# Set-up of a clustered-attention kernel: the first head pair's mask rows written by engines in place of transfers

## The chip, the cores and the metric

The kernel runs on one core of one Trainium2 chip. The metric is device time in microseconds (us) of one execution, the median of several runs; lower is better. The profile is of one execution of its own.

## What is computed

Clustered attention over 2 batches of 8 heads (768 positions, 64 wide), then two mixer blocks. Queries and keys are assigned to the nearest of 16 centroids, and a query sees only keys of its own cluster:

```
q_assign = np.argmax(np.einsum('bhsd,hcd->bhsc', q_n, c_n), axis=-1)
k_assign = np.argmax(np.einsum('bhsd,hcd->bhsc', k_n, c_n), axis=-1)
mask = q_assign[:, :, :, None] == k_assign[:, :, None, :]
scores = np.where(mask, scale * np.matmul(q, k.transpose(0, 1, 3, 2)), -1000000000.0)
attn = softmax(scores)
x = attn @ v                                  # then, with x as [batch, seq, 512]:
u = x + (x.T @ U @ V).T;  x = u + relu(u @ w_ch1) @ w_ch2
u = x + (relu(x.T @ w_tok1) @ w_tok2).T;  out = u + relu(u @ w_ch1') @ w_ch2'
```

## The kernel before

Heads are taken in pairs: 2 batches of 4 pairs, 8 pairs in all, and the head dimension of a pair lies on 128 partitions (head 0 on 0 to 63, head 1 on 64 to 127). float32 products are made of rounded high and low parts (`rnd`, line 75, writes the high part; `sub`, line 84, the low), and high and low rows are stacked into one contraction, so that a score tile takes two matmuls per half of the keys. For this each head of a pair has two operand tiles, `qS[g % 2][a]` and `kS[g % 2][a]` (a = head; the tiles lie in `qk0` and `qk1`, which the profile shows as qk). Rows 0 to 63 of a tile (for head 1, 64 to 127) hold the head itself; the other half holds 32 crossed rows at a time, copied there from other partitions by DMA (`cross`, line 253). Sixteen rows more carry the mask (`stack(..., "mask", ...)`, lines 270 to 273): a one-hot of the query's cluster on the query side, and 0 or -2^100 on the key side, so that a score of another cluster is pushed below every other.

The one-hots come from `scores` (line 193: centroids against q and k, four matmuls into one bank), `scores_out` (DVE transposes, tile am), `arg0` to `arg4` (lines 208 to 232: largest score, weights that settle a tie, compare, transpose into ohT) and `mask_rows` (line 234, into om), from which eight small DMAs per pair write the mask rows.

After `setup()` (line 390) the attention runs as 96 steps (`step`, line 659), 12 per pair, one score tile of 128 queries each. Step n issues the score matmuls of tile n+2 (`s_mm`), their maximum on DVE (`s_max`, line 294), the exponential of tile n+1 on ACT (`s_exp`, line 298), six transposes of tile n on PE (`t_mm`, line 313), their copies to pt (`t_out`, every third on DVE), and, from step 6 on, in odd steps the products with v (`pv`). A score bank is used again two tiles later, so the matmuls of tile n+2 wait for the exponential of tile n. Work for later pairs hangs on the steps by tables: `late[n]`, `acts[n]`, `low[n]`, `mid[n]` (line 588 on) are run at fixed places of step n. Every engine and every queue runs its instructions in the order in which they are written.

The second pair's raw q and k lie in pt (`raw1`, line 180, four blocks of 768 columns: raw q, high q, raw k, high k), which the softmax copies overwrite from step 6 on. SP's queue carries nearly all transfers, in program order: the first pair's crossed rows, the second pair's stack ("hi", "lo", "mask"), the third pair's load, v, then V and U (`load_uv`, line 497) and the weights. U is turned from 64-bit to float32 by ACT and DVE in place of the host (`uv`, line 502; on ACT at `acts[11]`, on DVE in `late[12]`).

`busy(n)` (line 447) issues n transposes of the identity into an unused bank.

## Time and profile before

| | |
|---|---|
| median of 3 runs | 754.79 us (754.76 to 754.88) |
| profiled execution | 754.72 us |
| its span in the profile | 752.9 us |
| PE busy | 739.8 us (98%) |
| DVE, ACT, POOL busy | 466.9, 311.6, 164.9 us |
| chain that ended last | PE 94%; DVE 2%; DMA, ACT, SP's queue 1% each |

The span is what the profile covers; the execution's own time is 1.8 us longer. Engines: PE makes matmuls and transposes, DVE, ACT and POOL work on elements, SP only issues transfers. Times within the execution count from the span's start. A line number in a row (L73) is that of the kernel before, often of a helper.

### The profile page before, as it was taken

What the parts mean: (1) busy time and instruction counts of PE and PEld (TensorE: products, weight loads), DVE (VectorE), ACT (ScalarE), POOL (GpSimd) and SP (SyncE); (2) the same over time, 40 slices, a digit from 0 to 9 for tenths busy, and PEclk for the clock granted to TensorE, in tenths of its full rate; (3) what the DMA queues carried; (4) which work ended last, traced back from release to release, by engine and by line L of the source; (5) the groups of instructions that cost most, each with busy time, mean ns of one, the idle gap of its engine ahead of it and who ended that gap; (6) DMA issues with size and microseconds to landing.
All of it is one profiled execution on the core that took longest, in us unless ns stands there. A gap on an engine that the chain in (4) does not pass through costs nothing.

```text
span 752.9 us, 10578 instructions
## 1 busy us (share of the span) xinstructions
PE 739.8 (98%) x3901; PEld 586.3 (78%) x3901; DVE 466.9 (62%) x690; ACT 311.6 (41%) x565; POOL 164.9 (22%) x145
## 2 busy tenths in 40 slices
PE   6999999999999999999999999999999999999998
PEld 4766766777776788888888888888888888888886
DVE  7788988878875567956667777567675331122113
ACT  5868778767776333322332334233232310101010
POOL 5132153232111122412212222136021410000000
PEclk9999999999999999999999999999999999999999
DMA  5797588785312354554433799878796538556652
GB/s 167 197 220 194 143 214 214 207 207 116 73 53 117 112 207 186 218 201 193 172 108 115 261 365 364 306 236 284 253 321 206 196 113 299 195 185 214 229 191 84
DMA packets 51715, 149.40 MB, mean 198 GB/s; under 512 B 7792, under 2 KB 15984, under 8 KB 49616
## 3 DMA queue, kind: packets, MB, share of 16 engines
q1 hardware_dynamic: 51104, 147.81, 61.4%
q10 hardware_dynamic: 560, 0.92, 0.4%
q8 instruction: 31, 0.51, 0.3%
q14 instruction: 20, 0.16, 0.1%
HBM read 97.32 MB, written 32.51 MB: 172 GB/s over the span
## 4 chain that ended last, share of the span: by engine, by line
PE 94%; DVE 2%; DMA 1%; ACT 1%; SPq 1%; issue 1%; DVEq 0%
PE ps L73 84%; PE ps L318 8%; PE ps L381 1%; PE ps L850 1%; PE ps L338 1%; DVE nm L296 1%; DMA sq__81<-in_qT_dram 1%; DMA qk<-pt 1%; ACT p L301 0%; SPq L256 0%; ACT pt L325 0%; DVE p L440 0%; ACT qk L78 0%; DVE u_sb L100 0%; SPq L263 0%
## 5 line engine op out<-in xcount | busy, mean ns | idle before, releaser
L754 DVE SCALAR_TENSOR_TENSOR gl<-ps,gh 128x512 fp32r<-128x512 f32 x84 | 58.0, 691 | 209.6 <-ACT gh L753 209.6
L753 ACT ACTIVATE gh<-ps 128x512 fp32r<-128x512 f32 x84 | 50.3, 598 | 312.8 <-PE ps L73 312.8
L73 PE MATMUL ps<-gh,qk 128*128 128x512 f32 x544 | 179.5, 391 | 0.1
L73 PEld LDWEIGHTS ps<-gh,qk 128*128 128x128 f32 x544 | 102.1, 188 | 21.6 <-issue 0.5
L73 PE MATMUL ps<-qk 112*128 112x384 f32 (+2 forms) x456 | 108.9, 365 | 1.4 <-DMA qk<-om 0.7
L296 DVE TENSOR_REDUCE nm<-ps 128x1 f32<-128x768 f32 x96 | 91.5, 955 | 28.2 <-PE ps L73 25.4
L73 PE MATMUL ps<-gl,qk 128*128 128x512 f32 x272 | 106.0, 390 | 0.0
L301 ACT ACTIVATE p<-ps,nm 128x768 f32<-128x768 f32 x96 | 86.1, 899 | 27.0 <-DVE nm L296 26.2
L85 POOL TENSOR_TENSOR qk<-c__77,qk 128x512 fp32r<-128x512 f32 x40 | 54.9, 1381 | 191.2 <-ACT qk L78 163.4
L318 PEld LDWEIGHTS ps<-ident,p 128*128 128x128 f32 x576 | 68.2, 140 | 34.0 <-issue 26.9
L318 PE MATMUL ps<-ident,p 128*128 128x128 f32 x576 | 91.2, 277 | 1.3 <-DVE pt L323 0.8
L73 PEld LDWEIGHTS ps<-qk 112*128 112x128 f32 (+1 forms) x456 | 76.2, 190 | 9.4 <-ACT p L301 3.6
L73 PE MATMUL ps<-u2h,qk 128*128 128x512 f32 x224 | 73.9, 391 | 0.0
L73 PE MATMUL ps<-pt,vr 128*64 128x384 f32 x384 | 72.1, 498 | 0.0
L325 ACT COPY pt<-ps 128x512 f32<-128x512 f32 x96 | 55.7, 587 | 26.9 <-PE ps L318 26.4
L73 PEld LDWEIGHTS ps<-gl,qk 128*128 128x128 f32 x272 | 51.1, 188 | 10.3
L73 PE MATMUL ps<-u1h,qk 128*128 128x512 f32 x160 | 52.6, 390 | 0.0
L100 DVE TENSOR_SCALAR c__77<-c__77 128x512 f32<-128x512 f32 (+2 forms) x47 | 48.9, 1041 | 0.8 <-ACT c__77 L96 0.7
L73 PEld LDWEIGHTS ps<-u2h,qk 128*128 128x128 f32 x224 | 42.1, 188 | 8.6
L109 DVE SCALAR_TENSOR_TENSOR c__77<-c__76,c__77 128x512 int32<-128x512 int32 (+2 forms) x47 | 43.4, 924 | 1.5
L106 DVE SCALAR_TENSOR_TENSOR c__77<-c__76,c__77 128x512 int32<-128x512 int32 (+2 forms) x47 | 43.5, 925 | 1.1
L73 PE MATMUL ps<-u2l,qk 128*128 128x512 f32 x112 | 43.6, 390 | 0.0
(153 smaller groups left out, 1027.1 us busy)
## 6 DMA issues: line engine op xcount, KB each, us to landing
qk<-scr_b SPq DMA_DIRECT2D x72, 512.0 KB, 3.5
c__76<-in_wa_dram SPq DMA_DIRECT2D x16, 1024.0 KB, 4.9
qk<-scr_a SPq DMA_DIRECT2D x32, 512.0 KB, 7.5
c__76<-in_wb_dram SPq DMA_DIRECT2D x24, 512.0 KB, 5.6
scr_b<-qk SPq DMA_DIRECT2D x24, 512.0 KB, 4.8
scr_a<-wx SPq DMA_DIRECT2D x16, 512.0 KB, 3.0
scr_a<-qk SPq DMA_DIRECT2D x16, 512.0 KB, 3.2
qk<-sq__81 SPq DMA_DIRECT2D x12, 384.0 KB, 4.1
```

Of the source, the lines that this page charges most:

```text
L73: pe.matmul(o, lhsT=l, rhs=r, start=start, stop=stop, **kw)
L85: eng.tensor_tensor(out=o, in0=a, in1=b, op=ALU.subtract)
L100: dve.tensor_scalar(out=dst, in0=dst, scalar1=2.0 ** -15, scalar2=122879.9921875, op0=ALU.max, op1=ALU.min)
L106: dve.scalar_tensor_tensor(out=d, in0=lo, scalar=29, in1=d, op0=ALU.logical_shift_right, op1=ALU.bitwise_or)
L109: dve.scalar_tensor_tensor(out=d, in0=hi, scalar=-0x40000000, in1=d, op0=ALU.bitwise_and, op1=ALU.bitwise_or)
L296: dve.tensor_reduce(out=nm[:, n % 4 : n % 4 + 1], in_=ps[:, b0 : b0 + 2, 0:HS], axis=AX.XY, op=ALU.max, negate=True)
L301: act.activation(p32[n % NP32].rearrange("p (j k) -> p j k", j=2), ps[:, b0 : b0 + 2, 0:HS], AF.Exp, bias=nm[:, n % 4 : n % 4 + 1], accum_ ...
L318: pe.transpose(ps[:, tb[j], ts(i, P)], p32[n % NP32][:, ts(c, P)], ident)
L325: act.copy(o, ps[:, tb[j], :])
L338: pe.transpose(ps[:, bk, ts(t, P)], osb[q % 2][:, ts(t, P)], ident)
L753: act.activation(gh, o, AF.Relu)
L754: dve.scalar_tensor_tensor(out=gl, in0=o, scalar=0.0, in1=f32(gh), op0=ALU.max, op1=ALU.subtract)
```

## The change

In `setup()`:

- The first pair's mask rows are no longer written to om and moved by eight DMAs. DVE (`k_row`) and ACT or POOL (`q_row`) write them straight from the transposed one-hots into the operand tiles, 16 partitions at a time.
- The end of the argmax is made for each head by itself: `eq` compares half the elements (one head's columns) into am3 or a new tile amb, of which the other half stays zero, and a transpose follows for each (ohT for head 0, ohb for head 1). Head 0's rows come first.
- Head 1's low parts of q and k go from DVE to POOL, behind a copy of one element (`turn`) that waits for head 0's last key row; POOL also scales raw q for it ahead.
- ACT rounds head 0's q in two pieces, with k between; the exponential's table is loaded ahead of the second pair's rounding, not behind it.
- Two of POOL's four fills go behind this work, the iota ahead of all of them.
- `busy` is issued in three places: 22 transposes as soon as the identity is there (before: none), 32 behind the cluster scores (44), 9 behind the first score matmuls (12).

In the tables of the steps: the second pair's `scores_out` and `arg0` move from the set-up to steps 0 and 1, head 1's second key row to step 0, the second pair's low parts, `arg2` to `mask_rows` and their DMAs from steps 0 to 3 to steps 4 to 6, and U and V from step 6 to 8. `raw1` takes its blocks in another order, so that the high parts are overwritten first.

```diff
-    raw1 = tuple(pt[:, 2 * NBL * P + i * S : 2 * NBL * P + (i + 1) * S] for i in range(4))
+    raw1 = tuple(pt[:, 2 * NBL * P + i * S : 2 * NBL * P + (i + 1) * S] for i in (2, 0, 3, 1))
...
+            busy(22)
             dve.memset(zc, 0.0)
-            for i in range(NST):
-                for t in (qS, kS):
-                    pool.memset(f32(t[i][1])[32:64], 0.0)
             wi = tmp.tile([P, 16], F32, name="wi")
             pool.iota(wi, pattern=[[-1, 16]], base=16, channel_multiplier=0, allow_small_or_imprecise_dtypes=True)
+            for t in (qS, kS):
+                pool.memset(f32(t[0][1])[32:64], 0.0)
+            amb = tmp.tile([P, HS], BF16, name="amb")
+            for x in (am3, amb):
+                dve.memset(x, 0.0)
...
-            for a in range(2):
-                m, _, _ = rows(a)
-                q, k = qS[0][a], kS[0][a]
-                rnd(act, q[m], Rq[m].unsqueeze(1).to_broadcast([64, 2, S]), 0.125)
-                rnd(act, k[m, 1, :], Rk[m])
-                if a == 0:
-                    cross(f32(k), f32(k[:, 1, :]), a, sp)
-                    low_q(0)
-                    low_k(0, pool)
-                else:
-                    cross(f32(k), f32(k[:, 1, :]), a, sp)
+            q, k = qS[0], kS[0]
+            pool.tensor_scalar(out=l[64:128], in0=Rq[64:128], scalar1=0.125, scalar2=None, op0=ALU.mult)
+            rnd(act, q[0][0:64, 0, :], Rq[0:64], 0.125)
+            rnd(act, k[0][0:64, 1, :], Rk[0:64])
+            rnd(act, q[0][0:64, 1, :], Rq[0:64], 0.125)
+            cross(f32(k[0]), f32(k[0][:, 1, :]), 0, sp)
+            dve.scalar_tensor_tensor(out=l[0:64].bitcast(F32R), in0=Rq[0:64], scalar=0.125, in1=f32(q[0][0:64, 0, :]),
+                                     op0=ALU.mult, op1=ALU.subtract)
+            cross(f32(q[0]), l, 0, sp)
+            sub(pool, k[0][0:64, 0, :], Rk[0:64], f32(k[0][0:64, 1, :]))
+            rnd(act, q[1][64:128], Rq[64:128].unsqueeze(1).to_broadcast([64, 2, S]), 0.125)
+            rnd(act, k[1][64:128, 1, :], Rk[64:128])
+            cross(f32(k[1]), f32(k[1][:, 1, :]), 1, sp)
+            act.activation(tiny, n1, AF.Exp, scale=0.0)
             scores(0)
             scores(1, raw1)
-            busy(44)
-            q_hi(raw1)
-            k_hi(raw1)
-            act.activation(tiny, n1, AF.Exp, scale=0.0)
+            busy(32)
             scores_out(0)
             arg0()
             arg1(dve)
             arg2()
-            arg3(dve)
-            arg4()
-            mask_rows(dve)
-            for a in range(2):
-                stack(0, a, "mask", (act, sp))
-            low_q(1)
-            low_k(1, dve)
-            for a in range(2):
-                stack(1, a, "hi", sp, raw1)
-            scores_out(1)
-            arg0()
-            arg1(pool)
-            k_lo(pool, raw1)
-            s_mm(0)
-            s_mm(1)
-            busy(12)
-            s_max(0)
-            s_max(1)
+            w3, wb_, v24 = (x.rearrange("p (g a c) -> p g a c", a=2, c=16) for x in (am3, amb, am2))
+            b24 = amx.rearrange("p (g a) -> p g a", a=2).unsqueeze(3).to_broadcast([P, 12, 2, 16])
+
+            def eq(o, a):
+                dve.tensor_tensor(out=o[:, :, 0, :], in0=v24[:, :, a, :], in1=b24[:, :, a, :], op=ALU.is_equal)
+
+            def k_row(a, oh, h):
+                y = rows(a)[2]
+                dve.tensor_scalar(out=k[a][y, 0, ts(h, HS)], in0=oh[64 + 32 * h : 80 + 32 * h], scalar1=-1.0, scalar2=BIG,
+                                  op0=ALU.add, op1=ALU.mult)
+
+            def q_row(eng, a, oh, h):
+                y = rows(a)[2]
+                o, i = q[a][y, 0, ts(h, HS)], oh[32 * h : 32 * h + 16]
+                if eng is act:
+                    act.activation(o, i, AF.Copy)
+                else:
+                    eng.tensor_copy(o, i)
+
+            eq(w3, 0)
+            dve.transpose(out=ohT, in_=am3)
+            for h in range(2):
+                k_row(0, ohT, h)
+                q_row(act, 0, ohT, h)
+            q_hi(raw1)
+            k_hi(raw1)
+            eq(wb_, 1)
+            dve.transpose(out=ohb, in_=amb)
+            pool.tensor_copy(tmp.tile([16, 1], F32, name="turn"), f32(k[0][96:112, 0, S - 1 : S]))
+            sub(pool, l[64:128].bitcast(F32R), l[64:128], f32(q[1][64:128, 0, :]))
+            cross(f32(q[1]), l, 1, sp)
+            q_row(pool, 1, ohb, 0)
+            sub(pool, k[1][64:128, 0, :], Rk[64:128], f32(k[1][64:128, 1, :]))
+            q_row(pool, 1, ohb, 1)
+            s_mm(0)
+            s_mm(1)
+            busy(9)
+            s_max(0)
+            s_max(1)
+            k_row(1, ohb, 0)
+            for a in range(2):
+                stack(1, a, "hi", sp, raw1)
+            late[0].insert(0, lambda: k_row(1, ohb, 1))
+            for t in (qS, kS):
+                pool.memset(f32(t[1][1])[32:64], 0.0)
+            k_lo(pool, raw1)
...
-    for s, f in ((0, lambda: q_lo(dve, raw1)), (1, arg2), (2, lambda: arg3(dve)), (2, arg4), (3, lambda: mask_rows(dve))):
+    for s, f in ((0, lambda: scores_out(1)), (1, arg0), (1, lambda: arg1(pool)), (4, lambda: q_lo(dve, raw1)), (5, arg2),
+                 (5, lambda: arg3(dve)), (6, arg4), (6, lambda: mask_rows(dve))):
```

On DVE, from the weights of the argmax to the second pair's first piece (am_83 is am, am_84 and am_85 are am2 and am3, qk_72 the first pair's operand tiles, nm the maxima), before:

```order
L222 TENSOR_REDUCE amx<-am_84 128x24
L229 TENSOR_TENSOR am_85<-am_84,amx 128x384
L232 STREAM_TRANSPOSE ohT<-am_85 128x384
L235 TENSOR_SCALAR om<-ohT,msk 128x384
L440 SCALAR_TENSOR_TENSOR p_3_94<-sq__81,qk_72 64x768
L85 TENSOR_TENSOR qk_72<-sk__82,qk_72 64x768
L201 STREAM_TRANSPOSE am_83<-ps 128x384
L209 TENSOR_REDUCE amx<-am_83 128x24
L296 TENSOR_REDUCE nm<-ps 128x1 x3
```

and with the change:

```order
L223 TENSOR_REDUCE amx<-am_84 128x24
L471 TENSOR_TENSOR am_85<-am_84,amx 128x12x16
L487 STREAM_TRANSPOSE ohT<-am_85 128x384
L475 TENSOR_SCALAR qk_72<-ohT 16x384 x2
L471 TENSOR_TENSOR amb<-am_84,amx 128x12x16
L494 STREAM_TRANSPOSE ohb<-amb 128x384
L297 TENSOR_REDUCE nm<-ps 128x1 x2
L475 TENSOR_SCALAR qk_72<-ohb 16x384
L297 TENSOR_REDUCE nm<-ps 128x1
```

Two low parts and the second pair's transpose and reduction have left the stretch ahead of the first maxima; head 1's key rows stand between maxima.

On POOL, from head 0's low k part to the second pair's argmax, before:

```order
L404 MEMSET qk_73 32x1536 x2
L406 IOTA wi 128x16
L85 TENSOR_TENSOR qk_72<-sk__82,qk_72 64x768
L85 TENSOR_TENSOR am_83<-am_83,amx 128x384
L215 TENSOR_SCALAR am_84<-am_83 128x384
L216 TENSOR_TENSOR am_84<-am_84,wcl 128x384
L85 TENSOR_TENSOR pt<-pt 128x768
```

and with the change:

```order
L447 TENSOR_SCALAR p_3_95<-sq__81 64x768
L85 TENSOR_TENSOR qk_72<-sk__82,qk_72 64x768
L495 COPY turn<-qk_72 16x1
L85 TENSOR_TENSOR p_3_95<-p_3_95,qk_72 64x768
L484 CAST qk_72<-ohb 16x384
L85 TENSOR_TENSOR qk_72<-sk__82,qk_72 64x768
L484 CAST qk_72<-ohb 16x384
L511 MEMSET qk_73 32x1536 x2
L85 TENSOR_TENSOR pt<-pt 128x768
L85 TENSOR_TENSOR am_83<-am_83,amx 128x384
```

POOL has a full row of work between the first pair's low k part and the second pair's argmax, where there was none.

On SP's queue, behind the second pair's high parts (qk_73 are that pair's tiles), before:

```order
L267 DMA qk_73<-pt 64x768
L256 DMA qk_73<-pt 32x768 x2
L267 DMA qk_73<-pt 64x768
L256 DMA qk_73<-pt 32x768 x2
L184 DMA sq__81<-in_qT_dram 128x768
L185 DMA sk__82<-in_kT_dram 128x768
L272 DMA qk_73<-om 16x384
```

and with the change:

```order
L185 DMA sq__81<-in_qT_dram 128x768
L186 DMA sk__82<-in_kT_dram 128x768
L190 DMA vr_91<-in_v_dram 128x6x128
L268 DMA qk_73<-pt 64x768
L257 DMA qk_73<-pt 32x768 x2
L268 DMA qk_73<-pt 64x768
L257 DMA qk_73<-pt 32x768 x2
L273 DMA qk_73<-om 16x384
```

The third pair's load and the second v, which stood before and behind the mask rows, now go ahead of the low parts; eight mask rows, V and U follow in both.

## Rows read from the trace of the kernel before

**Rows 1.** The page's busy time and share of each engine.

```profile
PE 739.8 (98%) x3901; PEld 586.3 (78%) x3901; DVE 466.9 (62%) x690; ACT 311.6 (41%) x565; POOL 164.9 (22%) x145
```

**Rows 2.** Chain of waits, 0 to 52 us: start, length, what it went through.

```profile
29.52 0.97 PE ps L73 x4
```

**Rows 3.** Timeline, DVE, set-up: start, length, line, operation, out<-in, count [idle before].

```profile
9.46 0.86 DVE L218 TENSOR_TENSOR am<-am,amx 128x384 bf16<-128x384 f32 x1
...
11.34 0.56 DVE L229 TENSOR_TENSOR am<-am,amx 128x384 bf16<-128x384 bf16 x1
11.93 0.58 DVE L232 STREAM_TRANSPOSE ohT<-am 128x384 bf16<-128x384 bf16 x1
12.54 0.48 DVE L235 TENSOR_SCALAR om<-ohT,msk 128x384 f32<-128x384 bf16 x1
13.05 0.95 DVE L440 SCALAR_TENSOR_TENSOR p<-sq__81,qk 64x768 fp32r<-64x768 f32 x1
...
16.50 1.82 DVE L296 TENSOR_REDUCE nm<-ps 128x1 f32<-128x768 f32 x2 [0.42 <-PE ps L73]
```

**Rows 4.** Timeline, POOL, set-up.

```profile
8.06 1.85 POOL L85 TENSOR_TENSOR qk<-sk__82,qk 64x768 fp32r<-64x768 f32 x1 [1.08 <-ACT qk L78]
...
17.09 1.18 POOL L215 TENSOR_SCALAR am<-am 128x384 bf16<-128x384 f32 x1
```

**Rows 5.** Timeline, PE, set-up.

```profile
9.43 5.28 PE L449 MATMUL ps<-ident 128*128 128x128 f32 x44
15.39 1.78 PE L73 MATMUL ps<-qk 112*128 112x384 f32 x8 [0.68 <-DMA qk<-om]
```

**Rows 6.** Timeline, ACT, set-up.

```profile
5.76 1.49 ACT L78 ACTIVATE qk<-sq__81 64x1536 fp32r<-64x1536 f32 x1 [2.02 <-DMA sq__81<-in_qT_dram]
...
11.83 1.28 ACT L467 ACT_TABLE_LOAD   x1
...
13.12 0.20 ACT L467 ACTIVATE tiny<-n 128x1 f32<-128x1 f32 x1
```

**Rows 7.** Busy time by stretch: length, then PE, PEld, DVE, ACT, POOL, PEclk, DMA.

```profile
16.50:31.00 14.50, 13.33 (x87) 11.12 (x85) 12.14 (x16) 10.30 (x22) 4.39 (x4) 1.00 0.88 202
```

**Rows 8.** Timeline, DVE, steps 0 and 12.

```profile
20.50 1.37 DVE L244 SCALAR_TENSOR_TENSOR pt<-pt 128x768 fp32r<-128x768 f32 x1
...
45.42 1.50 DVE L100 TENSOR_SCALAR u_sb<-u_sb 128x192 f32<-128x192 f32 x1
```

**Rows 9.** Timeline, POOL, beside the rows above.

```profile
19.23 1.83 POOL L85 TENSOR_TENSOR pt<-pt 128x768 fp32r<-128x768 f32 x1
...
44.97 1.84 POOL L85 TENSOR_TENSOR sk__82<-sk__82 128x768 fp32r<-128x768 f32 x1
```

**Rows 10.** Timeline, SP's queue: start and length of the issue.

```profile
15.55 1.17 SPq L256 DMA_DIRECT2D qk<-p  x2
...
29.59 0.51 SPq L272 DMA_DIRECT2D qk<-om  x1
...
34.68 0.58 SPq L189 DMA_DIRECT2D vr<-in_v_dram  x1
...
36.82 0.42 SPq L500 DMA_DIRECT2D xn<-in_U_dram  x1
```

**Rows 11.** Transfers issued, 0 to 50 us: count, KB each, median us to landing.

```profile
xn<-in_V_dram SPq DMA_DIRECT2D x3, 192.0 KB, 4.6
```

**Rows 12.** Timeline, ACT, steps 11 and 12.

```profile
42.09 0.39 ACT L96 ACTIVATE u_sb<-xn 128x192 f32<-128x192 f32 x1 [0.91 <-DMA xn<-in_U_dram]
42.38 0.89 ACT L301 ACTIVATE p<-ps,nm 128x768 f32<-128x768 f32 x1
```

**Rows 13.** Timeline, PE, steps 12 to 14.

```profile
43.49 0.95 PE L73 MATMUL ps<-qk 112*128 112x384 f32 x4
...
49.53 0.66 PE L318 MATMUL ps<-ident,p 128*128 128x128 f32 x4 [0.46 <-DVE pt L323]
50.43 0.66 PE L318 MATMUL ps<-ident,p 128*128 128x128 f32 x4 [0.25 <-ACT pt L325]
```

More of the change, by code (lines that the diff above doesn't have):

```diff
@@ L400, in setup, with busy @@
             make_identity(nc, ident)
+            def busy(n):
+                for i in range(n):
+                    pe.transpose(ps[:, 6, ts(i % 4, P)], ident, ident)
+            busy(22)
             dve.memset(zc, 0.0)
-            for i in range(NST):
-                for t in (qS, kS):
-                    pool.memset(f32(t[i][1])[32:64], 0.0)
             wi = tmp.tile([P, 16], F32, name="wi")
             pool.iota(wi, pattern=[[-1, 16]], base=16, channel_multiplier=0, allow_small_or_imprecise_dtypes=True)
+            for t in (qS, kS):
[3 more added lines that the diff above has]
+                dve.memset(x, 0.0)
             dve.memset(msk[0:64, 0:1], 0.0)
@@ L628, in tile_cluster_attention__then__two_mixers @@
         at(outs, s, lambda t=t: zadd_out(0, t, held["za"]))
-    for s, f in ((0, lambda: q_lo(dve, raw1)), (1, arg2), (2, lambda: arg3(dve)), (2, arg4), (3, lambda: mask_rows(dve))):
+    for s, f in ((0, lambda: scores_out(1)), (1, arg0), (1, lambda: arg1(pool)), (4, lambda: q_lo(dve, raw1)), (5, arg2),
+                 (5, lambda: arg3(dve)), (6, arg4), (6, lambda: mask_rows(dve))):
         at(late, s, f)
-    for what, s in (("lo", 1), ("mask", 3)):
+    for what, s in (("lo", 4), ("mask", 6)):
         for a in range(2):
             at(late, s, lambda a=a, w=what: stack(1, a, w, sp, raw1))
-    at(late, 6, load_uv)
+    at(late, 8, load_uv)
     for i, s0, ss in ((0, 11, (12, 12, 12, 12)), (1, 13, (14, 16, 18, 20))):
```

11 lines of the change are left out of this document (1 added, 10 removed).

## The prediction

> **What bounds the kernel now.** I read the page's shares first: PE is busy for 98% of the span [rows 1], and from about 29.5 us on the chain of waits runs through PE alone, the score matmuls of L73 first [rows 2]. So this change, which touches only the set-up and the steps of the first two pairs, can gain just what PE loses ahead of and in those steps, and keeps of it what no later wait takes back. Three waits matter, each read in the timeline of its engine.
>
> First, the start. DVE works through the argmax, the mask rows are ready at 13.02, and PE, which has been filling its time with 44 idle transposes, starts the scores at 15.39, held at last by a transfer of om; the first maximum starts at 16.50 [rows 3, 5].
>
> Second, steps 0 to 7. In the 14.50 us from the first maximum DVE is busy for 12.14, more than any engine but PE, whose time there holds overlaps and 12 idle transposes [rows 7].
>
> Third, step 12. ACT stands still for 0.91 us at U's transfer, which was issued at 36.82 and is used at 42.09: 5.27 us. The exponential behind it starts at 42.38, and the score matmuls that need its bank at 43.49, 1.40 us after U's arrival, with no idle time shown ahead of them [rows 10, 12, 13]. PE had nothing in hand there. **From here on PE cannot run earlier than U arrives plus 1.40 us**, however early it started.
>
> **The change, part by part.**
>
> *The start.* Up to the weights (11.30) DVE's list is the same. Its L218 took 0.86 us where the comparison over as many elements took 0.56, while POOL's L85 ran until 9.91 [rows 3, 4]: it waited some 0.3 for POOL. POOL's operation can now come somewhat sooner; I take nothing for it, with 0.3 of gain as the bound. Then, for head 0: half a comparison, between 0.28 and 0.56, taken as 0.32; a gap of 0.04; a transpose of 0.58; so 12.28. Two key rows of 384 elements on 16 partitions have no row of their own: the mask rows' 0.48 is the upper bound, the fixed 0.2 of a tiny operation the lower [rows 3, 6]; 0.35 each, so 13.0. ACT writes the query rows beside them, 0.5 each: 192 elements took 0.39 and 768 took 0.89 [rows 12]. First scores at about 12.95, for 15.39. DVE goes on with head 1's comparison and transpose, 0.32 and 0.62, so the first maximum starts at **14.0, 2.5 us earlier** than 16.50.
>
> The table load is moved ahead of this. In the trace it starts at 11.83, takes 1.28, and the next activation starts at 13.12, directly behind it [rows 6]. ACT's roundings for the first pair are as many elements as three operations of 1.49 us from 5.76 on [rows 6] and end near 10.3, load and activation near 11.8, so the query rows find ACT free and wait for nothing. The Trainium skill (ScalarE: Activation LUTs, "What ACT_TABLE_LOAD costs") adds a drain of about 1.38 us to each load. By that rule the query rows would start near 13.2, the first maximum near 14.9, and the sum would be 0.9 us worse than mine. The trace shows 0.01 us between load and activation, and I go by the trace.
>
> *Costing nothing.* The 22 early transposes run while PE waits for the centroids; 44 took 5.28 us [rows 5], so 22 end near 4.0, and at half that speed near 6.7. Even then the cluster scores' delay is mostly covered by POOL's operation, which holds L218 anyway; uncovered it costs 0.2. The new block order lets the copies of step 6 overwrite high parts whose transfers are issued by 24 us; if those were late, ACT would wait. Fewer idle transposes stand only in idle time.
>
> *DVE in the steps.* From first maximum to the second pair's mask rows DVE now does the 12.14 us of [rows 7], which hold the same kinds of work (eight maxima, three copies, the low part, the four ends of the argmax), plus a ninth maximum (0.91), two key rows (0.70), the transpose (0.58) and the reduction (0.56) that came out of the set-up, less 0.42 because the low part, 1.37 while POOL ran, should take the 0.95 of its like [rows 3, 8]: 14.5. To this come waits. Idle was 14.50 - 12.14 = 2.36; a key row now fills part of it, so 1.3 (between 0.5 and 2.36). And POOL, which was idle in this stretch up to the second pair's argmax, now works without a break from about 13 to 22 us: two low parts of 1.85, two copies, two fills, another low part. DVE's scalar operations can stand behind such an operation: L100 took 1.50, up to the end of POOL's 44.97 + 1.84 [rows 8, 9]. Both of head 1's key rows fall into that time. Each can wait between 0 and 1.85; I take 0.65 each, half of a mean operation: 1.3. Mask rows done at 14.0 + 14.5 + 1.3 + 1.3 = **31.1**. In step terms PE is then 1 to 2 us ahead of before.
>
> The Trainium skill (SBUF — State Buffer, "Who interferes with whom") has such operations take a port shared by DVE and POOL, copies and scalar operations within SBUF among them. The trace agrees for L100; for operations from bf16 to float32, as these key rows are, no row here shows it.
>
> *U.* SP issues the same transfers between the last crossed rows (15.55) and U as before: the load and v only change places with others. It can start when POOL's low part is done, near 15.0, so by its own work U would go out at 36.3. But the mask rows' eight transfers wait for DVE: before, SP came to them at 29.59 [rows 10]; now it would come there at about the same time and find them not made. From the first of them to U it took 7.23 us, 0.63 of it for v, which is no longer there [rows 10]: 6.60. So U is issued at 31.15 + 6.60 = 37.75. To landing it took 5.25; with v's 384 KB gone ahead of it, less: 4.3 to 5.25, near V's 4.6 [rows 11]; I take 4.5. U arrives at 42.25, **0.2 us later than before**, and what PE had gained is gone in one wait of ACT.
>
> *Given back.* At 49.53 and 50.43 PE idled 0.46 and 0.25, behind L100, which waited for POOL's third-pair operation at 44.97 [rows 8, 9, 13]. That operation follows the steps, which are ahead by then, and not U; so it should be over, and 0.7 us comes back.
>
> Sum: 0.7 - 0.2 = 0.5 us gained. Against the profiled execution's 754.72 that is 754.2; the median is 0.07 above it, so **754.3 us**.
>
> **The rivals.**
>
> *Faster: the load of U keeps up.* If the key rows do not wait for POOL and DVE's idle time is short, the mask rows end at 14.0 + 14.5 + 0.5 = 29.0, SP is the limit, U goes out at 36.3 and arrives by 40.6 to 41.5: 0.6 to 1.5 earlier, plus 0.7, so 752.5 to 753.4, say 752.9. For it: no row shows a bf16 operation of DVE waiting for POOL, and not all of the idle time need return. Against it: four pieces of DVE work were added or moved into a stretch that DVE bounds.
>
> *Slower: POOL takes its turn ahead of DVE's first low part.* The new scaling of raw q on POOL starts with the data, at 5.8 as ACT did [rows 6]. POOL's nearest rows are 1.18 for 384 elements, twice that for 768, or 2.4; a plainer operation may take half. Head 0's rounded k comes after two operations of half that 1.49, near 7.4. If the scaling lasts beyond that, over 1.6 us, POOL's 1.85 us subtraction [rows 4] stands ahead of DVE's low part, and with it of all DVE does after: some 2.1 us later up to U. Result 754.7 + 2.1 - 0.7 = 756.2. Against it: the start hides a few tenths, and the scaling has one input only.
>
> *It does not do what it says.* If head 0's crossed low rows, still transfers, landed after the engine-written rows, the start would be theirs. Their source is made ahead of the argmax, over 4 us before the key rows, and V's transfers, twice as large, took 4.6 [rows 11]; so this costs some tenths at most, unless the second rival holds them up too.
>
> *ACT not yet free.* If ACT needed another 1.4 us behind the table load, the query rows would start at 13.2 and all behind them 0.9 later: 755.2. The 0.01 us of [rows 6] speaks against it. It is the drain of the skill's page.
>
> *Only the sizes.* Both key rows waiting in full would put the mask rows at 33.5 and the time at 756.6.
>
> **How the numbers follow.** What differs by less than 0.2%, 1.5 us, cannot be told from no change here. The forecast, with its sizes off by 1 us either way, gets 0.58, nearly all of it inside that bound; the faster rival 0.27; the slower one 0.10; full waits 0.03; ACT not free 0.02. So faster by over 0.2%: 0.28, the faster rival's and a little of the forecast's; within: 0.60, with ACT not free in it; slower: 0.12, the slower rival's and most of the full waits'. The range reaches from the faster rival's end to the slower one's figure: 752.5 to 756.2.
>
> **What would show it.** The first score matmuls near 13 and the first maximum near 14 for the start. Key rows of over 1 us on DVE, ending with an operation of POOL, for the waits; mask rows near 31 and U issued near 37.8 for the limit. ACT's wait ahead of L96 should grow from 0.9 to 2 us or more, and the matmuls behind it start near 43.7. I am wrong if that wait is not longer (then the gain is kept, and the time is below 753), or if the first maximum comes after 15.5 (then POOL was in the way).

## The result, and the profile after the change

| | before | after the change |
|---|---|---|
| median, us | 754.77 (754.51 to 754.88, 6 runs) | 758.20 (757.84 to 760.28, 6 runs) |
| ratio, 95% interval | | 1.0052 [1.0039, 1.0065] |
| the profiled execution, us | 754.72, span 752.9 | 759.47, span 757.7 |

The change made the kernel 3.4 us slower. I had said 754.3 and a range up to 756.2: the prediction was wrong, in its direction too. The profiled execution of the changed kernel is 1.3 us above its median; the rows below are this execution's, and what varies between executions is told with kernels d, g and m. Lines of the new kernel up to L400 stand where they were or one further down, the set-up behind them (up to L512) is rewritten, and what follows stands 23 or 24 further down; in the kernels of the experiments a few lines more or less.

First the page's shares, beside [rows 1]: PE is as busy as before and the span is 4.8 us longer, so PE stood still longer or ran slower.

```profile
PE 744.7 (98%) x3908; PEld 592.9 (78%) x3908; DVE 468.5 (62%) x695; ACT 312.7 (41%) x568; POOL 171.6 (23%) x151
```

PE's timeline tells where (start, duration, operation; in brackets the idle time ahead and who ended it). The first scores are 2.6 us earlier than in [rows 5]. Then come two long idles, at tile 3 (21.20) and in step 12 (47.94). Before, step 12 has none [rows 13], and neither has tile 3, whose scores had this row:

```profile
20.15 0.95 PE L73 MATMUL ps<-qk 128*128 128x384 f32 x4
```

After the change:

```profile
12.81 1.63 PE L73 MATMUL ps<-qk 112*128 112x384 f32 x8 [0.60 <-ACT qk L482]
...
21.20 1.01 PE L73 MATMUL ps<-qk 128*128 128x384 f32 x2 [2.49 <-DVE qk L475]
...
47.94 1.65 PE L73 MATMUL ps<-qk 112*128 112x384 f32 x4 [2.32 <-ACT p L302]
```

The first idle was ended by DVE's second key row of head 1 (L475). Its timeline, to be read against [rows 3, 8]:

```profile
7.13 0.94 DVE L452 SCALAR_TENSOR_TENSOR p<-sq__81,qk 64x768 fp32r<-64x768 f32 x1
...
12.19 0.74 DVE L475 TENSOR_SCALAR qk<-ohT 16x384 fp32r<-16x384 bf16 x2
...
13.86 1.78 DVE L297 TENSOR_REDUCE nm<-ps 128x1 f32<-128x768 f32 x2
15.68 0.38 DVE L475 TENSOR_SCALAR qk<-ohb 16x384 fp32r<-16x384 bf16 x1
...
17.93 3.21 DVE L475 TENSOR_SCALAR qk<-ohb 16x384 fp32r<-16x384 bf16 x1
...
34.71 0.48 DVE L236 TENSOR_SCALAR om<-ohT,msk 128x384 f32<-128x384 bf16 x1
...
50.56 0.25 DVE L100 TENSOR_SCALAR u_sb<-u_sb 128x192 f32<-128x192 f32 x1
```

Four key rows of one shape: three took 0.37 to 0.38 us, the fourth 3.21. POOL's timeline beside it:

```profile
5.50 2.14 POOL L447 TENSOR_SCALAR p<-sq__81 64x768 f32<-64x768 f32 x1 [1.37 <-DMA sq__81<-in_qT_dram]
7.72 2.04 POOL L85 TENSOR_TENSOR qk<-sk__82,qk 64x768 fp32r<-64x768 f32 x1
...
15.35 0.50 POOL L484 CAST qk<-ohb 16x384 fp32r<-16x384 bf16 x1
15.92 1.82 POOL L85 TENSOR_TENSOR qk<-sk__82,qk 64x768 fp32r<-64x768 f32 x1
17.80 0.49 POOL L484 CAST qk<-ohb 16x384 fp32r<-16x384 bf16 x1
18.25 2.69 POOL L511 MEMSET qk<- 32x1536 f32 x2
```

The slow key row starts 0.3 us before the two fills and ends at 21.14, 0.2 after them (18.25 + 2.69 = 20.94). The third one, at 15.68, ran beside a cast and the start of a subtraction and lost nothing.

The second idle is U's. SP had nothing in hand ahead of the mask rows; they were made at 35.19, and V and U follow them. ACT (second fence) waits for U 3.57 us where it waited 0.91 [rows 10, 12]:

```profile
35.22 0.51 SPq L273 DMA_DIRECT2D qk<-om  x1
...
41.17 1.51 SPq L522 DMA_DIRECT2D xn<-in_V_dram  x3
42.72 0.42 SPq L523 DMA_DIRECT2D xn<-in_U_dram  x1
```

```profile
10.00 1.28 ACT L459 ACT_TABLE_LOAD   x1
11.30 0.20 ACT L459 ACTIVATE tiny<-n 128x1 f32<-128x1 f32 x1
12.19 1.07 ACT L482 ACTIVATE qk<-ohT 16x384 fp32r<-16x384 bf16 x2 [0.69 <-DVE ohT L487]
...
46.63 0.37 ACT L96 ACTIVATE u_sb<-xn 128x192 f32<-128x192 f32 x1 [3.57 <-DMA xn<-in_U_dram]
```

Last, the windows (a stretch and its length; busy time and number of instructions of PE, PEld, DVE, ACT and POOL; the granted clock, 1.00 being 2.4 GHz and 0.50 being 1.2, the DMA engines' busy share and GB/s). Behind each idle the granted clock goes to its lower level; before the change it was 1.00 over the first of these stretches [rows 7].

```profile
12.00:18.00 6.00, 4.67 (x31) 3.96 (x29) 4.92 (x10) 5.10 (x10) 4.64 (x5) 1.00 0.21 49
18.00:21.00 3.00, 0.58 (x2) 0.31 (x2) 3.00 (x1) 0.92 (x2) 2.93 (x3) 0.89 0.95 190
21.00:27.00 6.00, 5.80 (x22) 5.58 (x23) 3.79 (x6) 2.94 (x6) 4.12 (x4) 0.50 0.94 221
27.00:30.00 3.00, 2.87 (x20) 2.28 (x19) 2.58 (x4) 1.59 (x4) 0.64 (x1) 0.97 0.97 327
...
48.00:51.00 3.00, 3.00 (x13) 2.90 (x13) 1.27 (x3) 2.14 (x6) 0.65 (x1) 0.50 1.00 283
```

One table sums it up: how far the scores of a tile start behind (+) or ahead of (-) those of the kernel before, in us, in the profiled execution of each kernel (start of the tile's first L73 less the same in the trace of before). The letters are those of the experiments.

| kernel | tile 2 | 8 | 12 | 14 | 16 | 18 | 24 |
|---|---|---|---|---|---|---|---|
| the change | -2.68 | +1.80 | +1.88 | +4.44 | +5.94 | +4.78 | +4.80 |
| a, fills in the gap | -2.59 | -2.90 | -2.54 | +0.10 | +1.72 | +0.57 | +0.58 |
| b, V and U ahead of the low rows | -2.75 | +0.65 | +1.19 | +1.35 | +1.35 | +1.32 | +1.34 |
| c, a and b | -2.50 | -2.82 | +1.93 | +3.87 | +3.89 | +3.10 | +3.11 |
| d, first wait filled | -2.52 | -0.19 | +0.16 | +2.64 | +2.66 | +1.51 | +3.57 |
| e, a and U mid | -2.24 | -2.56 | -0.97 | -0.82 | -0.83 | -0.85 | -0.32 |
| f, e and wa later | -2.40 | -2.72 | -0.95 | -0.80 | -0.79 | -0.81 | -0.80 |
| g, before and U mid | +0.09 | +0.07 | +1.16 | +1.16 | +1.16 | +1.15 | +1.17 |
| h, the change and U mid | -2.55 | +1.84 | +1.93 | +1.93 | +1.93 | +1.90 | +3.67 |
| i, a, wa later, U between | -2.35 | -2.67 | -2.03 | -1.88 | -1.87 | -1.89 | -1.87 |
| j, a and wa later | -2.52 | -2.85 | -2.18 | +0.92 | +3.88 | +2.74 | +2.75 |
| k, j, second wait filled | -2.33 | -2.65 | -1.50 | +2.60 | +2.63 | +1.48 | +1.50 |
| l, before and wa later | -0.02 | -0.16 | -0.16 | +0.89 | +0.92 | -0.19 | -0.17 |
| m, i without a | -2.06 | +0.25 | +0.61 | +0.61 | +0.61 | +0.59 | +0.60 |
| n, i without the 22 | -2.60 | -2.94 | -1.99 | -1.84 | -1.82 | -1.85 | -1.84 |
| o, i with wa still later | -2.33 | -2.65 | -2.07 | -1.91 | -1.91 | -1.94 | -1.93 |
| p, o without the 22 | -1.87 | +0.27 | +0.34 | +0.34 | +0.34 | +0.32 | +0.34 |
| q, before and the 22 | +1.31 | +0.86 | +1.10 | +1.85 | +1.88 | +1.08 | +1.10 |

The change loses 4.5 us between tiles 2 and 8, 4.1 more at U between tiles 12 and 16, and gets 1.2 back behind.

### The profile page after: what moved, and what is told of

The parts are those of the page before. It is cut to its first block, busy times and chain, and to the rows that moved or that the text cites. A ratio compares the mean times of both kernels' runs of the same rounds, so it can differ in the third digit from the quotient of the medians.

```text
span 757.7 us, 10597 instructions
## 1 busy us (share of the span) xinstructions
PE 744.7 (98%) x3908; PEld 592.9 (78%) x3908; DVE 468.5 (62%) x695; ACT 312.7 (41%) x568; POOL 171.6 (23%) x151
## 4 chain that ended last, share of the span: by engine, by line
PE 94%; DVE 2%; ACT 1%; SPq 1%; issue 1%; DMA 1%; POOL 0%; DVEq 0%; POOLq 0%
PE ps L73 83%; PE ps L319 8%; DVE nm L297 1%; PE ps L382 1%; PE ps L874 1%; PE ps L339 1%; PE ps L405 1%; DMA xn<-in_U_dram 1%; SPq L274 0%; DVE qk L475 0%; ACT p L302 0%; SPq L273 0%; ACT pt L78 0%; ACT pt L326 0%; SPq L522 0%
## 5 line engine op out<-in xcount | busy, mean ns | idle before, releaser
L73 PE MATMUL ps<-gh,qk 128*128 128x512 f32 x544 | 179.5, 391 | 0.1
L73 PEld LDWEIGHTS ps<-gh,qk 128*128 128x128 f32 x544 | 102.1, 188 | 21.6 <-issue 0.5
L73 PE MATMUL ps<-qk 112*128 112x384 f32 (+2 forms) x456 | 111.5, 371 | 6.5 <-ACT p L302 3.0
L297 DVE TENSOR_REDUCE nm<-ps 128x1 f32<-128x768 f32 x96 | 91.6, 956 | 31.1 <-PE ps L73 25.3
L73 PE MATMUL ps<-gl,qk 128*128 128x512 f32 x272 | 106.0, 390 | 0.0
L319 PEld LDWEIGHTS ps<-ident,p 128*128 128x128 f32 x576 | 70.4, 144 | 32.4 <-issue 26.9
L73 PEld LDWEIGHTS ps<-qk 112*128 112x128 f32 (+1 forms) x456 | 78.0, 194 | 14.6 <-ACT p L302 5.6
L73 PE MATMUL ps<-u2h,qk 128*128 128x512 f32 x224 | 73.9, 391 | 0.0
L73 PE MATMUL ps<-pt,vr 128*64 128x384 f32 x384 | 72.1, 498 | 0.0
L73 PEld LDWEIGHTS ps<-gl,qk 128*128 128x128 f32 x272 | 51.1, 188 | 10.2
L73 PE MATMUL ps<-u1h,qk 128*128 128x512 f32 x160 | 52.6, 390 | 0.0
L100 DVE TENSOR_SCALAR c__77<-c__77 128x512 f32<-128x512 f32 (+2 forms) x47 | 48.9, 1041 | 0.8 <-ACT c__77 L96 0.7
L73 PEld LDWEIGHTS ps<-u2h,qk 128*128 128x128 f32 x224 | 42.0, 188 | 8.6
L73 PEld LDWEIGHTS ps<-pt,vr 128*64 128x64 f32 x384 | 23.5, 136 | 25.8 <-issue 25.6
```

Of the source, the lines that this page charges most:

```text
L73: pe.matmul(o, lhsT=l, rhs=r, start=start, stop=stop, **kw)
L100: dve.tensor_scalar(out=dst, in0=dst, scalar1=2.0 ** -15, scalar2=122879.9921875, op0=ALU.max, op1=ALU.min)
L297: dve.tensor_reduce(out=nm[:, n % 4 : n % 4 + 1], in_=ps[:, b0 : b0 + 2, 0:HS], axis=AX.XY, op=ALU.max, negate=True)
L319: pe.transpose(ps[:, tb[j], ts(i, P)], p32[n % NP32][:, ts(c, P)], ident)
```

## The experiments

Kernels d, k and q add idle transposes, n and p leave out the first 22. Each ratio is to the kernel before, run on the same chip.

**The wait of the key row, and U.** Kernel a moves the fills:

```
+            for t in (qS, kS):
+                pool.memset(f32(t[1][1])[32:64], 0.0)
             pool.tensor_copy(tmp.tile([16, 1], F32, name="turn"), f32(k[0][96:112, 0, S - 1 : S]))
...
             late[0].insert(0, lambda: k_row(1, ohb, 1))
-            for t in (qS, kS):
-                pool.memset(f32(t[1][1])[32:64], 0.0)
```

> POOL's two fills of the second set (L511, 2.69 us) are moved ahead of its 'turn' copy, into the 3.32 us in which it stood idle (9.76 to 13.08); nothing else changes. Theory 1, the second key row of head 1 waited for the two fills: it takes 0.4 to 1 us instead of 3.21, PE's idle of 2.49 us ahead of tile 3's second half is gone and with it the stretch at the lower clock, the scores of tile 4 start 3 us or more earlier than in the changed kernel, the second pair's mask rows end near 31 to 32 instead of 35.19, U is issued near 38 and lands near 42.5. Time 754 to 755. Theory 2, it waits for any operation of POOL: the row now stands behind the subtraction L85 that follows, takes 2.0 to 2.3 us, PE idles 1.3, mask rows near 34, time 756.5 to 757.5. Theory 3, DVE's own work sets the mask rows whatever the key row does: mask rows stay later than 34, time 757.5 or more.

Measured: 756.32 (755.33 to 757.10), 1.0023 [1.0014, 1.0032]. DVE:

```profile
18.03 0.58 DVE L475 TENSOR_SCALAR qk<-ohb 16x384 fp32r<-16x384 bf16 x1
...
30.29 0.48 DVE L236 TENSOR_SCALAR om<-ohT,msk 128x384 f32<-128x384 bf16 x1
```

PE and the windows of the same kernel:

```profile
43.59 1.65 PE L73 MATMUL ps<-qk 112*128 112x384 f32 x4 [2.39 <-ACT p L302]
```

```profile
21.00:27.00 6.00, 5.40 (x35) 4.58 (x35) 5.39 (x7) 5.22 (x12) 2.93 (x3) 1.00 0.96 222
38.00:43.50 5.50, 3.19 (x21) 1.80 (x18) 3.52 (x5) 1.80 (x5) 4.15 (x4) 1.00 1.10 271
43.50:48.00 4.50, 4.41 (x20) 4.11 (x22) 2.26 (x6) 3.65 (x8) 0.73 (x1) 0.62 0.98 208
```

Theory 1 is shown: the key row takes 0.58 though POOL's subtraction comes right behind it, so it was the fills; the mask rows end at 30.77, 4.4 us earlier, and the lead of the start lives to tile 12. But the time, said as 754 to 755, is a miss, and only 1.8 of the 3.4 us come back: U still stops PE for 2.39 us, and the slow clock behind that costs 1.6 more (table, tiles 14 to 16). Kernel b takes U's wait away and leaves the fills, kernel c does both:

```
+    at(late, 4, load_uv)
     for what, s in (("lo", 4), ("mask", 6)):
...
-    at(late, 8, load_uv)
```

> The loads of V and U are issued by SP right after v, ahead of the second pair's low rows; the key row still waits for the fills. Theory 1, U is the second of two places where time is lost: U is issued near 27.4, ACT's wait of 3.57 us ahead of L96 is gone, PE's idle of 2.32 us at 45.6 and the second stretch at the lower clock as well; the score matmuls stay 1.8 to 1.9 us behind those of the kernel before up to step 12, then 1.1 come back as in the changed kernel (L100 no longer waits), so 754.8 + 1.9 - 1.1 = 755.6, from 755.0 to 756.2. Rival, the mask rows' own landing or another operand of ACT holds step 12 as long: ACT still waits 2 us or more, time 757 to 758.

> Both edits. Theory 1: the start's lead of 2.6 us lives through steps 0 to 8 except for about 0.5 to 1 us, nothing takes it back at step 12, and 0.7 comes back at the two idles of step 14: 754.8 - 2 - 0.7 = 752.1, from 751.5 to 753. Rival, DVE's longer list in the steps takes the lead back by itself: the scores of tile 10 are level with those of the kernel before, and the time is 754 to 754.8.

Measured: b 756.19 (755.58 to 759.52), 1.0025 [1.0016, 1.0033], near the top of what the theory gave; ACT does not wait for U, the idle and the second slow stretch are gone, and the 1.1 us that I had counted back are not given back; they are made up for by a first slow stretch that is shorter than in the change (the window stands with kernel m below). c 757.85 (757.05 to 759.87), 1.0044 [1.0031, 1.0056]: a miss. Its lead of 2.8 us is lost in one stop between tiles 8 and 12, on ACT, and the slow clock behind that costs 1.9 more (table, tiles 12 to 14):

```profile
38.81 0.58 ACT L326 COPY pt<-ps 128x512 f32<-128x512 f32 x1 [5.60 <-DMA qk<-pt]
```

The copy overwrites a raw block whose low rows are still being transferred. In kernel a SP issued the last of these by 29.95; here V and U stand ahead of them and it is 34.82. The two edits do not add up, because an earlier PE meets a later transfer.

**The clock.** Kernel d puts 18 idle transposes where PE stood still at tile 3.

```
+    at(acts, 1, lambda: [pe.transpose(ps[:, 7, ts(i % 4, P)], ident, ident) for i in range(18)])
```

> The changed kernel with 18 idle transposes on PE ahead of tile 3's scores, where PE stood idle; all waits stay. Theory 1, the lower clock behind the idle (granted 0.50 from about 21 to 27, transposes 1.91 us for eight instead of 1.06) costs over 1 us on top of the wait: the granted clock stays near 1.0, the scores of tile 6 start 1 to 2 us earlier than in the changed kernel, and the time is 756 to 757.2. Rival, PE is not what bounds these steps, and the lower clock costs nothing: scores of tile 6 within 0.4 us of the changed kernel's, time 758 +- 0.4.

Measured: 757.90 (756.41 to 758.48), 1.0037 [1.0024, 1.0049]. The granted clock stays at 1.00 from 18 to 30 us:

```profile
21.00:27.00 6.00, 5.18 (x31) 4.12 (x32) 5.43 (x8) 3.52 (x7) 4.44 (x5) 1.00 0.94 215
```

Between tiles 2 and 8 the kernel loses 2.33 us, not 4.48: the slow clock was some 2.15 of it. Of the change's six executions none has a mean granted clock above 0.998; of d's five, four have 0.999 or more. The time hardly shows the gain: U's stop follows (2.48 us of lead), then one at tile 22, where ACT waits for the fourth pair's raw q. The theory's mechanism held; its time did not, and 757.90 is the rival's figure (758).

**The order of SP's transfers.** U alone ahead of the mask rows, with the fills moved (e), in the kernel before (g) and in the change (h); in f also the first block of wa (a mixer's weights), 1 MB, is asked for in step 14 in place of step 8:

```
-    at(late, 8, load_uv)
+    at(late, 8, load_v2)
+    at(late, 5, load_u)
...
-    early = [(8, 0, 1), (23, 0, 3), ...
+    early = [(14, 0, 1), (23, 0, 3), ...
```

> The fills in POOL's gap, and U's transfer alone (192 KB) issued between the second pair's low rows and its mask rows; V's three stay behind the mask rows. The run with V and U ahead of the low rows lost its lead at a copy of step 8 that had to wait for those low rows, which SP issued 5 us later. Theory: with the low rows left where they were, U goes out near 30, lands by 35, ACT does not wait ahead of L96, the lead of 2.5 us over the kernel before lives to step 14, and 0.7 comes back: 751.5 to 752.6. Rival, transfers in a crowded queue (mask rows, V, the 1 MB of wa, the third pair's rows) stop a step at another place whatever is moved: one idle of PE of 1.5 us or more after step 8, 753.5 to 755.5.

> As the run before, with wa's first block (1 MB) asked for in step 14 and not in step 8, so behind the third pair's high rows. If the crowded queue is what is left, SP's long issue near 45 (4 to 5 us) goes, the third pair's low rows and the fourth pair's loads go out 2 us or more earlier, and the time is 0 to 1 us below the run before and steadier (its runs within 0.5 us). If the queue stops nothing, the two are the same within 0.3 us.

> The kernel before the change, with U's transfer alone moved ahead of the second pair's mask rows. If U holds step 12 of the kernel before too, as its 0.91 us of ACT's wait says, up to 0.9 us are gained, 753.8 to 754.4; if the wait only overlaps what holds the step anyway (DVE), 754.7 +- 0.2.

> The changed kernel with U's transfer alone moved ahead of the second pair's mask rows, the fills where the change put them. As with both loads moved ahead of the low rows, ACT does not wait for U, PE does not idle there, and the scores stay 1.3 to 1.9 us behind the kernel before, of which 0.7 to 1.1 come back: 755.0 to 756.2. With the run that has the fills moved too, it says what the key row's wait for the fills costs when nothing behind takes it up: 3 to 4 us.

Measured: e 755.98, scattered from 753.27 to 760.82, 1.0028 [1.0009, 1.0047]: a miss, on the rival's side and beyond it; its profiled execution (754.41) has no single PE idle of 1.5 us, but loses 1.6 us of lead between tiles 8 and 12, idles of 0.32 and 0.77 among it. f 753.80 (753.05 to 754.82), 0.9986 [0.9977, 0.9994]: 2.2 us below e and steadier, though not within the 0.5 us that was expected, and the first that beats the kernel before. g 757.54 (755.82 to 758.94), 1.0033 [1.0023, 1.0043]: a miss by 3 us. h 758.32 (756.62 to 761.08), 1.0047 [1.0033, 1.0060]: a miss; U's wait is gone and nothing is gained. First g's, then h's row of ACT:

```profile
33.24 0.84 ACT L78 ACTIVATE sq__81<-sq__81 128x768 fp32r<-128x768 f32 x1 [1.32 <-DMA sq__81<-in_qT_dram]
```

```profile
64.25 0.84 ACT L78 ACTIVATE sq__81<-sq__81 128x768 fp32r<-128x768 f32 x1 [2.41 <-DMA sq__81<-in_qT_dram]
```

In g the third pair's load stands behind U and stops step 8. The profiled execution, 755.87, shows this stop alone; five of the ten executions, 758.13 to 758.94, have a mean granted clock of 0.998 besides. In h the fourth pair's load, issued at 60.60 (in the kernel before at 56.37), stops PE for 1.32 us at tile 22. So U is only the first of a row of transfers that all follow the mask rows; in the changed kernel they are all late together, and taking one out of the row leaves the next.

**Putting the row in order.** In i U goes between the mask rows of head 0 and those of head 1; j is f without a move of U; k is j with 20 idle transposes ahead of the scores that wait for U; l is the kernel before with wa later.

```
             at(late, s, lambda a=a, w=what: stack(1, a, w, sp, raw1))
+            if what == "mask" and a == 0:
+                at(late, s, load_u)
...
-    at(late, 8, load_uv)
+    at(late, 8, load_v2)
```

> Fills in POOL's gap, wa's first block asked for in step 14, and U's transfer between the four mask rows of the first half (which step 10 needs) and the four of the second. In the run with U ahead of all eight, PE idled 0.5 and 0.8 us at steps 8 and 10 and its lead fell from 2.45 to 0.95 us: the mask rows came later by U. Theory, SP's order of transfers is all that is left: the lead of 2.5 us lives through step 10, U lands near 37.5 and stops nothing, and the time is 751.5 to 753. Rival, the lead is lost at the next transfer in the row (second half's mask rows, V, the fourth pair's loads): 753.3 to 754.3, as without this edit.

> Fills in POOL's gap and wa's first block in step 14; U where the change has it, behind the mask rows and V. If the crowd behind U is what makes the run with the fills alone 1 us slower in most of its executions than in the profiled one, this is 755.0 to 755.6 and steady; PE idles about 2.4 us for U near 41, the clock halves behind it and the scores go from 2.5 us ahead to 0.5 us behind the kernel before. Rival, the crowd does nothing here: 756.3.

> As the run before, with 20 idle transposes on PE in step 12 ahead of the scores that wait for U, so that PE does not stand still there; the wait for U stays. If the lower clock behind the wait costs 1.4 us by itself (in the run with the fills alone the scores lost 2.64 us at the wait and 1.42 more in the slow stretch behind it), the granted clock stays near 1.0 there and the time is 1.0 to 1.6 us below the run before. Rival, the lower clock costs nothing since DVE or ACT set the pace there: within 0.4 us of the run before.

> The kernel before the change with wa's first block asked for in step 14 alone. It tells how much of what the other versions gain by that edit is the change's: if the crowded queue stops the kernel before nowhere, 754.8 +- 0.3; if it gains there too, 754.0 to 754.4.

Measured: i 753.59 (752.80 to 756.31), 0.9987 [0.9978, 0.9996]: the rival's figure in the median, the theory's in the profiled execution, 752.82, which keeps 1.9 of the 2.35 us. j 755.92 (753.65 to 758.89), 1.0014 [1.0001, 1.0026]: not the steady run that was expected. k 754.77 (754.11 to 757.67), 1.0008 [0.9998, 1.0018]: 1.15 us below j, as its theory says. l 754.77, 1.0000 [0.9991, 1.0008]: wa's place is worth nothing to the kernel before. For the clock, PE and one window of j, then of k:

```profile
44.41 1.65 PE L73 MATMUL ps<-qk 112*128 112x384 f32 x4 [2.70 <-ACT p L302]
```

```profile
44.40:50.00 5.60, 5.59 (x20) 4.76 (x22) 2.95 (x6) 3.98 (x8) 0.34 (x1) 0.50 1.04 219
```

```profile
46.10 0.98 PE L73 MATMUL ps<-qk 112*128 112x384 f32 x4 [1.52 <-ACT p L302]
```

```profile
46.00:50.00 4.00, 3.90 (x26) 2.95 (x26) 2.72 (x6) 3.94 (x9) 0.00 (x0) 1.00 1.05 215
```

In j the scores fall back another 2.96 us between tiles 14 and 16, in the slow stretch; in k, where U came 1.7 us later still, by 0.03. So the slow clock behind U's wait costs between 1.5 us (the change, kernel a) and 3 us, and nothing where it does not fall, as in k. That the transposes kept it up in k is likely and not shown: in d PE idled 2.24 us at U, with no transposes there, and the clock stayed at 1.00. In the medians the difference is 1.15, but the intervals of j and k overlap.

**The key row's wait alone, the early transposes, the rest.** m is i with the fills back where the change put them, n is i without the 22 early transposes, o is i with wa's block in step 17, behind the fourth pair's loads.

> The changed kernel with SP's new order only (U between the two halves' mask rows, wa's first block in step 14), the fills back where the change put them. It prices the second key row's wait alone, with nothing behind it that takes it up or adds to it. Theory: PE idles 2.5 us ahead of the second half of tile 3, runs at the lower clock for some 6 us behind it, and loses 4.4 us between tiles 2 and 8 (from 2.7 ahead to 1.8 behind the kernel before), none of which comes back: 753.6 + 4.4 less what was still lost behind in that run, 756.2 to 757.5. Rival, PE's slack in steps 8 to 12 takes part of it back: 754.8 to 755.8.

> The fastest version so far (fills in POOL's gap, U between the mask rows, wa in step 14) without the 22 transposes at the very start. I had priced them at nothing; the trace of the change has the cluster scores at 0.52 us for two instead of 0.86, and the centroids' transpose 0.56 later. If they are worth what they save (0.2 to 0.4 us of the start), 753.8 to 754.1; if nothing, 753.6 +- 0.3; if the clock of the first scores hangs on them, 754.5 or more.

> The fastest version so far with wa's first block asked for in step 17, behind the fourth pair's two loads and no longer just ahead of them. If the executions of 754 us and more of that version come from those loads landing late, they go: median 752.7 to 753.2 and all within 0.6 us of each other. Rival, they come from the clock or from transfers ahead of U: the same spread as before, 753.6.

Measured: m 755.72 (754.86 to 756.68), 1.0010 [1.0001, 1.0019]; below the theory's range and inside the rival's. n 755.92 (753.80 to 757.11), 1.0010 [1.0002, 1.0019]. o **753.00** (752.50 to 753.98), 0.9975 [0.9966, 0.9984], the fastest of all, as expected in the median, though its executions lie within 1.5 us and not 0.6. Its interval overlaps that of i, so wa's second move is not shown to gain.

In m's profiled execution the clock did not fall, though PE idled as long as in the changed kernel (2.49 us). Its DVE row and its window, and the same window of kernel b:

```profile
18.55 3.21 DVE L475 TENSOR_SCALAR qk<-ohb 16x384 fp32r<-16x384 bf16 x1
```

```profile
21.00:27.00 6.00, 4.72 (x28) 3.69 (x29) 5.45 (x8) 3.08 (x7) 4.45 (x5) 1.00 0.95 198
```

```profile
21.00:27.00 6.00, 5.88 (x28) 5.25 (x29) 4.44 (x7) 2.95 (x6) 4.45 (x4) 0.72 0.96 224
```

It lost 2.31 us between tiles 2 and 8, as d did; i gains 0.32 there. The wait by itself is thus some 2.3 to 2.6 us, and the other 2.2 of the change's 4.5 are the clock. Kernel b, with the same key row and a mean clock of 0.72 in this window for the change's 0.50, lies between: 3.40. What I took for slack giving something back was the missing slow stretch. m's three executions with a mean granted clock of 1.000 took 754.86 to 755.28 us, its eight with 0.995 to 0.998 took 755.38 to 756.68. In n the trace shows i's lead at every tile, and 2.5 us lost behind the attention: 1.2 where PE waits once, 0.95 us, for weights, and 1.3 behind the last matmul, where the last transfers of the output end later. The key rows are as short as in i (0.36 and 0.55), so what n loses is not lost in the start. Two more runs ask further: p is o without the 22, q the kernel before with them.

> The fastest version (fills in POOL's gap, U between the mask rows, wa in step 17; 753.0, all executions with a mean granted clock of 0.999 to 1.000) without the 22 transposes at the very start. If these keep the clock, this one falls into two kinds of executions, those at a mean clock of 0.997 to 0.998 some 2 us slower, median 754.5 to 756. If the slow executions of the earlier run without them came from wa's place, 753.0 +- 0.4.

> The kernel before the change with the 22 early transposes added and nothing else. Its executions have a mean clock of 0.999 to 1.000 as it is, so nothing is to be kept: 754.8 +- 0.3. If the transposes set the start by more than that (cluster scores at 0.52 us for two instead of 0.86), up to 0.3 us less; if they hold up the centroids' transpose, up to 0.5 more.

Measured: p 755.33 (752.56 to 757.43), 1.0000 [0.9982, 1.0018]; q 755.54 (754.58 to 756.06), 1.0003 [0.9987, 1.0019]. By the medians p is 0.5 us above the kernel before (754.80 on that chip) and q 0.7. p is as slow as n, so it is not wa's place. Its profiled execution, 756.06, loses its lead in two places. The first is the start. PE's rows, with o's 32 idle transposes to compare in the second fence:

```profile
9.40 4.50 PE L405 MATMUL ps<-ident 128*128 128x128 f32 x32
13.65 1.64 PE L73 MATMUL ps<-qk 112*128 112x384 f32 x8
...
20.61 0.61 PE L73 MATMUL ps<-qk 128*128 128x384 f32 x2 [1.75 <-DVE qk L474]
```

```profile
8.77 3.71 PE L405 MATMUL ps<-ident 128*128 128x128 f32 x32
```

Without the early ones the 32 last until 13.9 here, hold up the first scores by 0.5 us, and shift DVE against POOL. Both of head 1's key rows then fall into POOL's subtractions (DVE, then POOL):

```profile
16.48 1.61 DVE L474 TENSOR_SCALAR qk<-ohb 16x384 fp32r<-16x384 bf16 x1
...
19.11 1.44 DVE L474 TENSOR_SCALAR qk<-ohb 16x384 fp32r<-16x384 bf16 x1
```

```profile
16.06 1.82 POOL L85 TENSOR_TENSOR qk<-sk__82,qk 64x768 fp32r<-64x768 f32 x1
17.94 0.51 POOL L483 CAST qk<-ohb 16x384 fp32r<-16x384 bf16 x1
18.54 1.81 POOL L85 TENSOR_TENSOR pt<-pt 128x768 fp32r<-128x768 f32 x1
```

PE idles, the clock falls behind it (0.72 from 21 to 27), and 2.1 us of lead are gone by tile 8. The key rows' price hangs on some tenths of a microsecond of phase.

The second place is the one of n: 0.9 us go where PE waits for weights near the end (first fence). SP issues the output ahead of these weights, and that takes 5.62 us in p (second fence) for 3.77 in o (third):

```profile
695.78 0.47 PE L73 MATMUL ps<-gh,qk 128*128 128x512 f32 x1 [0.61 <-DMA qk<-scr_b]
```

```profile
686.00 5.62 SPq L806 DMA_DIRECT2D out_dram<-xn  x8
```

```profile
683.73 3.77 SPq L807 DMA_DIRECT2D out_dram<-xn  x8
```

In n it takes 5.60; in all other traces, that of the kernel before among them, 3.76 to 3.80. So leaving out the 22 also changes something far behind the start, and no run says what. q gains nothing, and in its profiled execution loses: its 44 transposes end earlier, PE idles 1.75 us where the scores still wait for om, and the clock falls.

## Why the prediction was wrong, step by step

*Costing nothing: wrong for the 22 transposes.* Without them n and p are some 2 us slower than i and o. I had only asked whether they end in time (the 22 ended at 6.31, for "near 4.0" or "near 6.7"). How they are worth so much stays open: p's trace loses 2.1 us in the phase of the key rows, n's nothing there, and both lose about 1 us at the weights.

*The start: right.* First scores at 12.81 (12.95 said), first maximum at 13.86 (14.0), key rows 0.37 (0.35), query rows 0.53 each (0.5). The table load began 0.01 us behind the rounding ahead of it and took 1.28, the next activation began 0.02 behind it, and ACT then idled 0.69 before the query rows: by these rows the drain of the Trainium skill (ScalarE: Activation LUTs, "What ACT_TABLE_LOAD costs") is not there, as I had taken it, and the rival that stood on it is out.

*The slower rival: its condition came true and its effect did not.* POOL's scaling lasted 2.14 us, beyond the 1.6 from which I let it decide. But DVE's low part (7.13, 0.94 us) did not wait for the subtraction: it started beside the end of the scaling (7.64) and took what its like take, and the subtraction (7.72) took 2.04 for 1.85.

*DVE in the steps: the step that failed.* "Each can wait between 0 and 1.85; I take 0.65 each, half of a mean operation: 1.3." The first did not wait, the second waited 2.83 (3.21 less 0.38). The bound was one POOL operation; I had listed the two fills just ahead of it and did not ask whether DVE gets its turn between them. In p, where each row meets one subtraction, they wait 1.23 and 1.06, inside the bound. In the sum for the mask rows, 14.0 + 14.5 + 1.3 + 1.3 = 31.1, the terms measured 13.86 + 14.85 + 3.65 + 2.83 = 35.19: the waits were put 1.5 us too small and the idle time 2.35, of which the clock (next) made 1.8. With the wait gone (kernel a) the mask rows end at 30.77, with 14.95 us of work and 1.87 idle: near the 31.1, in part by luck, since the idle time was 0.6 longer than said and the waits 1.1 shorter. The range was also too narrow for the prediction's own words: "Both key rows waiting in full" gave 756.6, beyond its end of 756.2.

*The clock: missing in the sum.* I priced waits by their length. Where PE stood still for 1.75 to 3.5 us the granted clock mostly fell to 0.50 behind it for 3 to 7 us, and in the change that cost nearly as much again: 2.2 us at tile 3, 1.5 at U. In the first place it also makes the mask rows later, since DVE waits for slower scores: its idle time from the first maximum to the mask rows went from 1.9 us (kernel a) to 21.33 - 17.68 = 3.65. In m, where the key row waits as long and the clock stays up, it is 19.44 - 17.59 = 1.85.

*U: right in kind, late by what failed above.* From first mask row to U it took 7.50 us (6.60 said), to landing 3.9 (4.5), so 46.63 is 4.4 us after the 42.25 of the prediction; scores at 47.94 for "U plus 1.40", 48.03. The sign "ACT's wait ahead of L96 should grow from 0.9 to 2 us or more" came true in kernel a too (3.65), with the scores at 43.59 for the 43.7 said. So even without the fills there was no gain to be had, and with the clock's 1.6 and 0.5 more given back (below) the sum for kernel a is a loss of 0.6, as its profiled execution shows.

*Given back: right in place.* L100 took 0.25 us for 1.50, and 1.2 us came back (0.7 said). But b, h and i, where U is early, get nothing back, though i's steps are 1.9 us ahead: L100 took 1.48 to 1.50 in them. It was U's lateness that let POOL's operation pass first, and not, as I wrote, that the steps were ahead.

The account of the profiled execution: 0.5 gained by the sum; U 4.4 later, less 0.1 by which the scores came sooner behind it; the clock behind U 1.5; 0.5 more given back than said: -0.5 + 4.3 + 1.5 - 0.5 = 4.8, the span's difference.

## What to carry to other kernels

Where an engine's small operation is put into a stretch in which another engine works without a break, bound its wait by the whole run of operations behind which it can stand, not by one; then move that run to where the other engine idles (here POOL had 3.3 us free, and the fills fitted). A lead at the start is worth nothing until each transfer that the later steps need is also earlier: write down SP's row from the late step to the last transfer that follows it, and reorder it as a whole; a single transfer moved ahead cost the kernel before 2.7 us in the median. And price a PE idle such as these at up to twice its length, or fill it.
